# Mask products of two score steps issued together in four 32-row groups, in a routed-attention and hard-swish kernel

## Chip, cores and metric

The kernel runs on one core of one Trainium2 chip. The metric is the device time of one execution in microseconds, the median of several executions. The engines have the names of the profile: PE is the matrix engine (PEld its loads of weights), DVE the vector engine, ACT the scalar engine, POOL the third elementwise engine, SP the engine that issues most of the DMA transfers.

## What is computed

Routed attention over 4 batches of 8 heads, 768 positions, 64 dimensions per head, followed by a two-layer block with a hard-swish. A query sees the keys of its own cluster alone; the cluster of a row is the one of 16 normalised centroids with the largest product.

```python
q_assign = np.argmax(np.einsum('bhsd,hcd->bhsc', q_n, c_n), axis=-1)
k_assign = np.argmax(np.einsum('bhsd,hcd->bhsc', k_n, c_n), axis=-1)
mask = q_assign[:, :, :, None] == k_assign[:, :, None, :]
scores = np.where(mask, scale * np.matmul(q, k.transpose(0, 1, 3, 2)), -1000000000.0)
attn = np.exp(scores - np.max(scores, axis=-1, keepdims=True))
attn = attn / (np.sum(attn, axis=-1, keepdims=True) + 1e-09)
x = np.matmul(attn, v)            # then (B, H, S, D) -> (B*S, H*D) = (3072, 512)
h = x @ w_in                      # w_in is 512 x 2048
out = (h * np.clip(h + 3.0, 0.0, 6.0) / 6.0) @ w_out
```

## The kernel before

The 32 heads are handled as 16 pairs (`g`): two heads of a pair lie in the two halves of the 128 partitions, `t` = 0 in rows 0 to 63 and `t` = 1 in rows 64 to 127. The first eight pairs (`FIRST` = 8) are "unsorted": their scores are taken in full, 768 by 768, and masked. The last eight are sorted by cluster first and take only bands of the scores; they have their own functions (`band_scores` and others) and are not touched by the change.

The unsorted pairs run in 96 steps `n`, 12 for a pair: step `n` handles one half of the queries (`hf`, 384 of them) and one chunk of 128 keys (`j`) for both heads. Its scores stand in a PSUM tile `ps` of two banks, one bank per head. `psum_s` has two such tiles, so the tile of step n is the one that step n-2 had, and is free when the exponential of step n-2 has read it.

The mask is added to the scores by a product of its own. `route` makes one-hot rows of the clusters (`one_hot`, 128 positions by 12 chunks by 128 columns, of which each head uses 16 out of 64), where a query's row has a one in its cluster and a key's row has ones everywhere else; `route_turn` turns these rows on PE into `xm`, whose rows are clusters and whose columns are positions, the keys' part scaled by -2^60. The product of `xm`'s keys and queries is then 0 for a pair of one cluster and -2^60 for others. It is bfloat16 and has 64 rows per head. The product of the queries and keys themselves (`xf`) is fp32 and also has 64 rows per head. In the profile each fp32 matmul appears as two records, a bf16 one as one record.

`scores(n)` issues, for one step, the two mask products (one per head, `start=True`) and the two score products onto the same banks (`stop=True`). In the first step of a pair (`hf == j == 0`) the score products come first, through `scores_qk`, since `xm` is not ready yet; for the first pair that holds for steps 0 and 1.

The main loop takes two steps at a time (`for n in range(0, total + lag_d + 2, 2)`), and everything is issued in the order in which it is written (`manual_schedule`): each engine works through its own instructions in that order. A round of the loop holds, in this order: `scores`, `exponentials` (ACT, L423) and `key_sums` (POOL, L433) of steps n and n+1; `attn_v` (L443) of steps n-2 and n-1; every sixth step the sum over keys and its reciprocal (`sum_up`, L467, L473); then preparation for the next pair, by the round's place `r` in its pair: `turn` (transposes of q and k, L320) at r = 0 and 2, `cluster_scores` (L337) at r = 4, `route` (L348 to L357) at r = 6, `route_turn` (L379) at r = 8 and 10; and steps that decode the weights of the two layers from their 64-bit form (L228 to L259), mostly on DVE, some on ACT. From step 56 on, products of the first layer for a finished batch (L597) are put between the rounds. After the 96 steps comes the long part (the sorted pairs between the products of the two layers, L645 and L684), which lasts until the end.

The functions that the change touches are `route`, `scores` and, new, `masks`.

Of the kernel before, what the change touches and what calls it, by code (L numbers as in the profile page):

```python
# [8 lines left out]
F32 = mybir.dt.float32  # L9
# [4 lines left out]
ACT = mybir.ActivationFunctionType  # L14
# [3 lines left out]
C = 16  # L18
P = 128
NCH = S // P  # L20
NC2 = 2 * NCH
HALF = S // 2
NHC = NCH // 2
# [96 lines left out]
def fast_path(ctx, tc, ok, q, k, v, centroids, moe_w_in, moe_w_out, out):  # L120
# [3 lines left out]
    nc = tc.nc  # L124
# [32 lines left out]
    psum_s = whole.enter_context(tc.tile_pool(name="psum_s", bufs=2, space=PSUM))  # L157
# [10 lines left out]
    one_hot = nump.tile([P, NC2, P], BF16, name="one_hot")  # L168
# [9 lines left out]
    st = {}  # L178
    later = []

    def scratch(shape, name, dtype=F32):

        if st["early"]:
            return psum_m.tile(shape, dtype, name=name, tag="m")
        return psum_t.tile(shape, dtype, name=name, tag="t")
# [158 lines left out]
    def route(g):  # L344
        cs = st.pop(("cs", g))
        pr = scratch([P, NC2, 2, C], "pr")
        for i in range(NC2 // 4):
            nc.tensor.transpose(out=pr[:, 4 * i : 4 * i + 4], in_=cs[:, i], identity=ident)  # L348
        pr = pr.rearrange("p j t c -> p (j t) c")
        mx = rtp.tile([P, 2 * NC2], F32, name="mx")  # L350
        nc.vector.reduce_max(out=mx, in_=pr, axis=AX.X)
        oh = one_hot.rearrange("p j (t c) -> p j t c", t=2)[:, :, :, 0:C]
        pr = pr.rearrange("p (j t) c -> p j t c", t=2)
        mx = mx.rearrange("p (j t) -> p j t", t=2)
        halves = [slice(0, NCH), slice(NCH, NC2)]
        for sl, op in zip(halves, (ALU.is_ge, ALU.is_lt)):
            nc.vector.tensor_tensor(  # L357
                out=oh[:, sl], in0=pr[:, sl],
                in1=mx[:, sl].unsqueeze(3).to_broadcast([P, NCH, 2, C]), op=op,
            )  # L360


        def count():
            for a, sl in enumerate(halves):
                seen = rtp.tile([P, NCH, 2, C], BF16, name="seen")
                nc.scalar.activation(
                    out=seen, in_=oh[:, sl], func=ACT.Copy, scale=1.0 - 2 * a,
                    accum_out=counts[:, a, g : g + 1],
                )

        later.append(count)
# [16 lines left out]
    def where(n):  # L388
        g, r = divmod(n, 2 * NCH)
        return (g, *divmod(r, NCH))  # L390

    def scores_qk(n):
        st["ps", n] = psum_s.tile([P, 2, 512], F32, name="ps")
        scores_part(n, st["xf", where(n)[0]], True, False)

    def scores_part(n, x, first, last, onto=False):
        g, hf, j = where(n)
        for t in range(2):
            r = slice(t * D, (t + 1) * D)
            nc.tensor.matmul(  # L400
                st["ps", n][:, t, 0:HALF], lhsT=x[r, NCH + j],
                rhs=x[r, hf * NHC : (hf + 1) * NHC], start=first, stop=last,
                skip_group_check=onto,
            )

    def scores(n):
        g, hf, j = where(n)
        if ("ps", n) not in st:  # L410
            if hf == j == 0:
                scores_qk(n)
            else:
                st["ps", n] = psum_s.tile([P, 2, 512], F32, name="ps")
                scores_part(n, st["xm", g], True, False)
                scores_part(n, st["xf", g], False, True)
                return
        scores_part(n, st["xm", g], False, True)

    def exponentials(n):  # L420
        sc = st.pop(("ps", n))[:, :, 0:HALF]
# [772 lines left out]
    def prep_items(g, r):  # L1194

        if g > FIRST:
            return []
        turns = [lambda part=part: turn(g, part) for part in range(3)]
        if g == FIRST:
            return {  # L1200
                0: turns[:2], 2: turns[2:], 4: [lambda: cluster_scores(g)], 6: [lambda: own_clusters(g)],
            }.get(r, [])
        one_hots = [lambda: route_turn(g, 0), lambda: route_turn(g, 1)]
        return {
            0: turns[:2], 2: turns[2:], 4: [lambda: cluster_scores(g)], 6: [lambda: route(g)],
            8: one_hots[:1], 10: one_hots[1:],
        }.get(r, [])
# [38 lines left out]
    with tc.manual_schedule():  # L1246
# [12 lines left out]
        cluster_scores(0)  # L1259
        scores_qk(0)  # L1260
        route(0)
        scores_qk(1)
        for part in range(2):
            route_turn(0, part)

        for n in range(0, total + lag_d + 2, 2):
            g, r = divmod(n, per_pair)
            steps = [i for i in (n, n + 1) if i < total]
            prep = prep_items(g + 1, r)
            for i in steps:  # L1270
                scores(i)
                exponentials(i)
                key_sums(i)
# [359 lines left out]
@with_exitstack  # L1633
def kernel(
    ctx: ExitStack,
    tc: tile.TileContext,
    q: bass.AP,
    k: bass.AP,
    v: bass.AP,
    centroids: bass.AP,  # L1640
    moe_w_in: bass.AP,
    moe_w_out: bass.AP,
    out: bass.AP,
):
    ins = (q, k, v, centroids, moe_w_in, moe_w_out)
    flagp = ctx.enter_context(tc.tile_pool(name="flagp", bufs=1))
    ok = flagp.tile([1, 1], I32, name="ok")
    with ExitStack() as inner:
        good = fast_path(inner, tc, ok, *ins, out)
    with tc.If(good == 0):  # L1650
        with ExitStack() as inner:
            general_path(inner, tc, *ins, out)
# [32 lines left out]
```

## Time and profile before

| | us |
|---|---|
| median of three executions | 969.6 |
| lowest and highest of them | 968.26, 972.77 |
| the profiled execution | 966.25 |
| span of the profiled execution, first to last instruction | 964.5 |
| PE busy | 937.2 |
| DVE busy | 593.6 |
| POOL busy | 575.9 |
| ACT busy | 351.7 |

The profile is of one execution. "Busy" is the union of an engine's instructions in time. A row of a group of instructions has the source line, the engine, the operation, what it writes and reads, the tile of the matrix engine in use (64*128 is 64 rows by 128 columns), the shapes, the count, then the time in us covered by the group and the mean duration of one in ns, and last the time that the engine stood idle just before such instructions, with what ended it. A row of the timeline has the start in us, the length in us, the engine, the instruction, the count of instructions merged into the row, and in brackets the idle time before it. Matmuls overlap in their pipeline, so a row's length is longer than the time until the next can start: the distance of two starts is the time that a group takes on PE.

### The profile page before, as it was taken

What the parts mean: (1) busy time and instruction counts of PE and PEld (TensorE: products, weight loads), DVE (VectorE), ACT (ScalarE), POOL (GpSimd) and SP (SyncE); (2) the same over time, 40 slices, a digit from 0 to 9 for tenths busy, and PEclk for the clock granted to TensorE, in tenths of its full rate; (3) what the DMA queues carried; (4) which work ended last, traced back from release to release, by engine and by line L of the source; (5) the groups of instructions that cost most, each with busy time, mean ns of one, the idle gap of its engine ahead of it and who ended that gap; (6) DMA issues with size and microseconds to landing.
All of it is one profiled execution on the core that took longest, in us unless ns stands there. A gap on an engine that the chain in (4) does not pass through costs nothing.

```text
span 964.5 us, 17602 instructions
## 1 busy us (share of the span) xinstructions
PE 937.2 (97%) x6358; PEld 724.8 (75%) x6358; DVE 593.6 (62%) x1306; ACT 351.7 (36%) x715; POOL 575.9 (60%) x1302
## 2 busy tenths in 40 slices
PE   8999999999899999999999999899999999999997
PEld 5444445455798797797887888778788799999996
DVE  6789888989985375384483473464473464626261
ACT  6888887865112232232132141241231311202020
POOL 3878767657366577877777868767787150303030
PEclk9999999999999999999999999999999999999999
DMA  7345454340474467375583574753744333323220
GB/s 200 95 132 154 132 175 128 107 138 11 157 234 121 119 180 157 103 193 123 165 201 100 141 177 128 169 138 102 185 145 108 99 97 112 105 70 106 58 64 26
DMA packets 174351, 124.23 MB, mean 129 GB/s; under 512 B 134064, under 2 KB 152496, under 8 KB 174256
## 3 DMA queue, kind: packets, MB, share of 16 engines
q1 hardware_dynamic: 164320, 109.86, 42.7%
q0 software_dynamic: 9216, 12.60, 4.3%
q8 instruction: 52, 0.85, 0.4%
q10 hardware_dynamic: 720, 0.56, 0.2%
q14 instruction: 43, 0.35, 0.1%
HBM read 94.67 MB, written 28.31 MB: 128 GB/s over the span
## 4 chain that ended last, share of the span: by engine, by line
PE 62%; POOL 4%; DMA 3%; DVE 3%; issue 1%; ACT 0%; SPq 0%; DVEq 0%; POOLq 0%; ACTq 0%
PE Y L684 16%; PE uY L645 13%; PE X L684 11%; PE uX L645 10%; PE ps L1060 4%; PE pv L1080 3%; DMA piece<-qd 3%; PE ps L899 2%; POOL kvd L1014 1%; POOL qd L1014 1%; POOL w_low L1006 1%; DVE tx L556 1%; PE pd L1104 1%; PE ps L1121 1%; DMA xn<-xsd,pos 0%
## 5 line engine op out<-in xcount | busy, mean ns | idle before, releaser
L433 POOL TENSOR_TENSOR acc<-acc,ex 128x768 f32<-128x768 f32 x64 | 123.4, 1927 | 37.4 <-ACT ex L423 33.9
L1014 POOL DMA_INDIRECT qd<-qn,pos x96 | 96.9, 1010 | 62.3 <-DVE pos L997 22.3
L1030 POOL DMA_INDIRECT xn<-xsd,pos x96 | 93.8, 977 | 46.5 <-ACT sx L499 25.1
L499 ACT ACTIVATE sx<-g_sb,half_c 128x512 f32<-128x512 f32 x88 | 63.5, 721 | 141.2 <-DVE g_sb L656 137.2
L635 POOL TENSOR_TENSOR g_sb<-g_sb 128x256 f32<-128x256 f32 x52 | 41.8, 824 | 122.1 <-DVE g_sb L502 121.1
L1014 POOL DMA_INDIRECT kvd<-kvn,pos x96 | 95.8, 998 | 26.1 <-issue 26.1
L1006 POOL MEMSET w_low<- 128x1 f32 x864 | 91.1, 105 | 33.3
L691 DVE TENSOR_TENSOR y<-y,Y 128x256 f32<-128x256 f32 x48 | 20.2, 421 | 132.3 <-PE Y L684 131.5
L684 PE MATMUL X<-w_out_sb,g_sb 128*128 128x256 f32 x384 | 90.5, 382 | 4.0 <-DVE y L691 2.2
L645 PE MATMUL uX<-xb,w_in_sb 128*128 128x128 f32 x704 | 93.0, 275 | 0.0
L684 PE MATMUL Y<-w_out_sb,g_sb 128*128 128x256 f32 x384 | 89.0, 381 | 0.0
L684 PE MATMUL Y<-T,g_sb 128*128 128x256 f32 x384 | 88.7, 381 | 0.0
L645 PEld LDWEIGHTS uX<-xb,w_in_sb 128*128 128x128 f32 x704 | 85.7, 192 | 0.0
L684 PEld LDWEIGHTS X<-w_out_sb,g_sb 128*128 128x128 f32 x384 | 70.9, 190 | 17.6 <-issue 3.1
L684 PEld LDWEIGHTS Y<-T,g_sb 128*128 128x128 f32 x384 | 71.8, 190 | 13.2 <-issue 4.0
L684 PEld LDWEIGHTS Y<-w_out_sb,g_sb 128*128 128x128 f32 x384 | 71.6, 190 | 12.8 <-issue 3.8
L400 PE MATMUL ps<-xf 64*128 64x384 f32 x384 | 78.5, 487 | 0.7 <-ACT ex L423 0.7
L656 DVE TENSOR_TENSOR sx<-uX,sx 128x128 f32<-128x128 f32 x176 | 51.0, 290 | 43.2 <-ACT sx L663 31.0
L423 ACT ACTIVATE ex<-ps 128x768 f32<-128x768 f32 x96 | 72.6, 803 | 4.6 <-PE ps L400 4.5
L443 PE MATMUL pv<-ex,vt 128*64 128x384 f32 x384 | 72.5, 499 | 0.0
L1064 ACT ACTIVATE be<-ps 128x768 f32<-128x768 f32 (+1 forms) x48 | 35.5, 739 | 88.9 <-PE ps L1060 57.7
L656 DVE TENSOR_TENSOR g_sb<-uY,sx 128x128 f32<-128x128 f32 (+1 forms) x176 | 65.6, 415 | 0.0
(186 smaller groups left out, 1803.4 us busy)
## 6 DMA issues: line engine op xcount, KB each, us to landing
tx<-td SPq DMA_DIRECT2D x86, 384.0 KB
raw<-in_moe_w_in_dram SPq DMA_DIRECT2D x16, 512.0 KB
raw<-in_moe_w_out_dram SPq DMA_DIRECT2D x16, 512.0 KB
xb<-xd SPq DMA_DIRECT2D x12, 512.0 KB
out_dram<-y SPq DMA_DIRECT2D x44, 128.0 KB
qk<-in_q_dram SPq DMA_DIRECT2D x18, 192.0 KB
qk<-in_k_dram SPq DMA_DIRECT2D x18, 192.0 KB
vt<-in_v_dram SPq DMA_DIRECT2D x16, 192.0 KB
```

The source lines that it names most:

```text
L400: nc.tensor.matmul(st["ps", n][:, t, 0:HALF], lhsT=x[r, NCH + j], rhs=x[r, hf * NHC : (hf + 1) * NHC], start=first, stop=last, skip_group_ ...
L423: nc.scalar.activation(out=ex, in_=sc, func=ACT.Exp, scale=SM_SCALE)
L433: nc.gpsimd.tensor_tensor(out=acc, in0=acc, in1=ex, op=ALU.add)
L443: nc.tensor.matmul(pv[t * D : (t + 1) * D], lhsT=vt[:, t, j], rhs=ex[:, t], start=(j == 0), stop=(j == NCH - 1),)
L499: nc.scalar.activation(out=r, in_=h, func=ACT.Relu, bias=half_c, scale=1.0 / 6.0)
L635: eng.tensor_tensor(out=out_, in0=in0, in1=in1, op=op)
L645: nc.tensor.matmul(dst, lhsT=w[:, kt], rhs=x(kt), start=(kt == 0), stop=(kt == HK - 1))
L656: nc.vector.tensor_tensor(out=out_, in0=in0, in1=in1, op=ALU.add)
L684: nc.tensor.matmul(bank[:, half * HC : (half + 1) * HC], lhsT=g_sb[:, kind, i], rhs=w[:, i], start=(first and i == 0), stop=(last and i == ...
L1006: nc.gpsimd.memset(w_low, W_LOW)
L1014: i = nc.gpsimd.indirect_dma_start(out=rows[name, g, t], in_=src, in_offset=None, out_offset=bass.IndirectOffsetOnAxis(ap=pos[:, a, j, t : ...
L1030: nc.gpsimd.indirect_dma_start(out=xn[:, j, t], out_offset=None, in_=rows["xsd", g, t], in_offset=bass.IndirectOffsetOnAxis(ap=pos[:, 0, j ...
```

## The change

`one_hot` keeps its size. Its 128 columns per chunk were two blocks of 64, one per head, with 16 in use; they become four blocks of 32, two copies `d` of (head 0, head 1), again with 16 in use each. `route` writes each of its two comparisons twice, once for each copy. After `route_turn`, which is unchanged, `xm` has the rows of head 0 at 0 to 31 and 64 to 95, those of head 1 at 32 to 63 and 96 to 127.

A new function `masks(n)`, called in the even steps, issues the mask products of steps n and n+1 together: four matmuls of 32 rows, each in a row group of its own and into a bank of its own. For this it takes the PSUM tile of step n+1 already at step n, before the score products of step n. Then `scores(n)` issues the score products of step n and `scores(n + 1)` those of step n+1. Where the score products came first (`scores_qk`), the masks are added behind them, as before.

```diff
@@ route
-        oh = one_hot.rearrange("p j (t c) -> p j t c", t=2)[:, :, :, 0:C]
+        oh = one_hot.rearrange("p j (d t c) -> p j d t c", d=2, t=2)[:, :, :, :, 0:C]
...
         for sl, op in zip(halves, (ALU.is_ge, ALU.is_lt)):
-            nc.vector.tensor_tensor(
-                out=oh[:, sl], in0=pr[:, sl],
-                in1=mx[:, sl].unsqueeze(3).to_broadcast([P, NCH, 2, C]), op=op,
-            )
+            for d in range(2):
+                nc.vector.tensor_tensor(
+                    out=oh[:, sl, d], in0=pr[:, sl],
+                    in1=mx[:, sl].unsqueeze(3).to_broadcast([P, NCH, 2, C]), op=op,
+                )
...
                 nc.scalar.activation(
-                    out=seen, in_=oh[:, sl], func=ACT.Copy, scale=1.0 - 2 * a,
+                    out=seen, in_=oh[:, sl, 0], func=ACT.Copy, scale=1.0 - 2 * a,
                     accum_out=counts[:, a, g : g + 1],
                 )
@@ scores
+    def masks(n):
+        for d in range(2):
+            g, hf, j = where(n + d)
+            begun = ("ps", n + d) in st
+            if not begun:
+                st["ps", n + d] = psum_s.tile([P, 2, 512], F32, name="ps")
+            x = st["xm", g]
+            for t in range(2):
+                r = slice((2 * d + t) * 2 * C, (2 * d + t + 1) * 2 * C)
+                nc.tensor.matmul(
+                    st["ps", n + d][:, t, 0:HALF], lhsT=x[r, NCH + j],
+                    rhs=x[r, hf * NHC : (hf + 1) * NHC], start=not begun, stop=begun,
+                )
+            st["masked", n + d] = not begun
+
     def scores(n):
         g, hf, j = where(n)
-        if ("ps", n) not in st:
-            if hf == j == 0:
+        if n % 2 == 0:
+            if hf == j == 0 and ("ps", n) not in st:
                 scores_qk(n)
-            else:
-                st["ps", n] = psum_s.tile([P, 2, 512], F32, name="ps")
-                scores_part(n, st["xm", g], True, False)
-                scores_part(n, st["xf", g], False, True)
-                return
-        scores_part(n, st["xm", g], False, True)
+            masks(n)
+        if st.pop(("masked", n)):
+            scores_part(n, st["xf", g], False, True)
```

## Prediction

> **What bounds the kernel now.** I read the page's totals first, then the busy time by stage, then the matmul groups by shape, then the timeline of PE around the score steps.
>
> ```profile
> span 964.5 us, 17602 instructions
> PE 937.2 (97%) x6358; PEld 724.8 (75%) x6358; DVE 593.6 (62%) x1306; ACT 351.7 (36%) x715; POOL 575.9 (60%) x1302
> ```
>
> ```profile
> 60.00:84.40 24.40, 24.27 (x165) 10.78 (x165) 23.25 (x27) 20.95 (x47) 18.89 (x10) 1.00 0.54 151
> ...
> 240.00:600.00 360.00, 351.96 (x2452) 293.48 (x2449) 211.56 (x573) 93.17 (x175) 255.47 (x764) 1.00 0.58 154
> 600.00:965.00 365.00, 353.96 (x2434) 313.76 (x2432) 177.19 (x490) 77.70 (x152) 155.41 (x436) 0.99 0.39 105
> ```
>
> The columns are the stretch, its length, then busy time of PE, PEld, DVE, ACT, POOL. PE is busy throughout, so time on PE counts one for one. The first row is one unsorted pair: PE 24.27 of 24.40, but DVE 23.25 and ACT 20.95 too, so here the order of waits between three engines matters. The change lies wholly in this first quarter.
>
> ```profile
> L400 PE MATMUL ps<-xf 64*128 64x384 f32 x384 | 78.5, 487 | 0.7 <-ACT ex L423 0.7
> L400 PE MATMUL ps<-xm 64*128 64x384 bf16 x192 | 30.5, 327 | 3.2 <-ACT xm L384 1.3 <-ACT ex L423 1.0 <-DVE xm L382 0.7
> ```
>
> Today PE waits hardly at all before score and mask products (0.7 and 3.2 us in all).
>
> **What is removed.** One round of two steps on PE:
>
> ```profile
> 119.85 0.85 PE L337 MATMUL pcs<-xf,cnT 128*32 128x384 f32 x8
> 120.64 0.34 PE L400 MATMUL ps<-xm 64*128 64x384 bf16 x2
> 120.81 0.81 PE L400 MATMUL ps<-xf 64*128 64x384 f32 x4
> 121.45 0.33 PE L400 MATMUL ps<-xm 64*128 64x384 bf16 x2
> 121.61 0.81 PE L400 MATMUL ps<-xf 64*128 64x384 f32 x4
> 122.35 1.51 PE L443 MATMUL pv<-ex,vt 128*64 128x384 f32 x8
> ```
>
> From start to start, the two mask products of a step, side by side in two row groups of 64, take 121.61 - 121.45 = 0.16 us together. If four groups of 32 run side by side as two do, a round needs 0.16 once, not twice: 48 rounds x 0.16 = 7.7 us less. No row shows four row groups. The row nearest to it is the first of this fence: eight fp32 records in four column groups take 0.79 us, two records each at 0.32 (half of 0.64, below) plus a changeover, so four column groups do run at once. I take four row groups as one, and keep two at a time (nothing removed) as the other end.
>
> **What is added on PE: a change of tile shape.** Score products of one step take 121.45 - 120.81 = 0.64 when the mask products of the same shape follow. When `pv` of another shape (128*64) follows, 122.35 - 121.61 = 0.74. So a change of shape holds PE for 0.10 us. Behind a change the first weights are not loaded ahead either, as the first step of a pair shows, where score products come directly after transposes:
>
> ```profile
> 58.94 0.92 PE L400 MATMUL ps<-xf 64*128 64x384 f32 x4
> 59.91 0.50 PE L400 MATMUL ps<-xm 64*128 64x384 bf16 x4
> 60.25 0.81 PE L400 MATMUL ps<-xf 64*128 64x384 f32 x4
> 60.99 1.51 PE L443 MATMUL pv<-ex,vt 128*64 128x384 f32 x8
> ```
>
> 0.92 against 0.81: 0.11 us for fp32 weights. Now the masks are 64*128 like the scores, and the step from one to the other is free. Behind the change the masks are 32*128 and the scores 64*128: one changeover more per round, 0.10 + 0.11 = 0.21 us, in 47 rounds (in the first, scores come before both masks): 9.9 us. In a pair's first round the extra change from scores to masks falls into the wait for `xm` (58.94 to 59.91 is 0.97, not 0.74). That no row has 32-row groups leaves the ends 0 (no changeover between row groups) and about 0.3 (four weight loads of the masks one behind the other, 0.03 us each by a row shown below, 0.11 for four). I take 0.21, as rows of three other shapes agree on the 0.10.
>
> [...]
>
> Balance on PE alone: +9.9 - 7.7 = **+2.2 us**.
>
> **What is moved: the wait for the exponential.** `masks(n)` writes the tile of step n+1, which the exponential of step n-1 must have left. Before, PE asked for that 0.8 us later, behind the score products of step n. Everything on PE is queued behind it: score products, `pv`, transposes. ACT is often late, since decoding and copies stand before its exponentials. The release itself takes 0.05 us:
>
> ```profile
> 123.91 1.49 ACT L423 ACTIVATE ex<-ps 128x768 f32<-128x768 f32 x2
> ...
> L423 ACT ACTIVATE ex<-ps x96: 787/799/856, 14.3 to 234.4; 128x768 f32<-128x768 f32 x96
> ```
>
> ```profile
> 124.75 0.34 PE L400 MATMUL ps<-xm 64*128 64x384 bf16 x2 [0.41 <-ACT ex L423]
> ```
>
> The first of the two exponentials ends at 123.91 + 0.79 = 124.70, and PE, which waited, starts at 124.75. The second ends at 125.40: the new wait here is 125.40 + 0.05 - 124.75 = 0.70. Two more, from one pair:
>
> ```profile
> 59.05 0.81 ACT L384 ACTIVATE xm<-po 128x768 bf16<-128x768 bf16 x1 [0.57 <-PE po L379]
> 62.53 1.49 ACT L423 ACTIVATE ex<-ps 128x768 f32<-128x768 f32 x2
> 71.93 0.48 ACT L342 COPY cs<-pcs 128x384 f32<-128x384 f32 x1 [1.11 <-PE pcs L337]
> 74.27 1.49 ACT L423 ACTIVATE ex<-ps 128x768 f32<-128x768 f32 x2
> ```
>
> ```profile
> 63.45 0.34 PE L400 MATMUL ps<-xm 64*128 64x384 bf16 x2
> 75.43 0.34 PE L400 MATMUL ps<-xm 64*128 64x384 bf16 x2
> ```
>
> 62.53 + 1.49 + 0.05 - 63.45 = 0.62, and 74.27 + 1.49 + 0.05 - 75.43 = 0.38. Both can fall due in one pair, for ACT's work is tied to PE: at 59.05 and again at 71.93 ACT had idled until PE gave it `po` and `pcs`, and is busy without a gap from there to the exponentials. A PE that is later makes ACT later by as much. (Between the two, at 67.85, a lack of 0.48 is covered by the 0.62 just lost.) Over the 48 rounds I find 12 such waits; the first and the last:
>
> ```profile
> 14.31 1.51 ACT L423 ACTIVATE ex<-ps 128x768 f32<-128x768 f32 x2 [0.52 <-PE ps L400]
> 190.16 1.49 ACT L423 ACTIVATE ex<-ps 128x768 f32<-128x768 f32 x2
> ```
>
> ```profile
> 15.39 0.34 PE L400 MATMUL ps<-xm 64*128 64x384 bf16 x2
> 191.37 0.34 PE L400 MATMUL ps<-xm 64*128 64x384 bf16 x2
> ```
>
> 0.48 and 0.33. Worked out alike for the rest (0.11, 0.33, 0.45, 0.33, 0.60, 0.70, 0.45), the 12 sum to 5.5 us. PE arrives some 0.05 us later in each by its own balance: **+4.9 us**. Ends: 2 us, if ACT catches up more between the waits; 7.4 us without the changeover, for then PE arrives 0.21 earlier at each.
>
> **What is added on DVE.** Two comparisons more per pair:
>
> ```profile
> 12.02 0.62 DVE L357 TENSOR_TENSOR one_hot<-pr,mx 128x192 bf16<-128x192 f32 x2
> 13.32 0.56 DVE L382 TENSOR_SCALAR xm<-po 128x768 bf16<-128x768 bf16 x1 [0.67 <-PE po L379]
> ...
> 78.70 0.62 DVE L357 TENSOR_TENSOR one_hot<-pr,mx 128x192 bf16<-128x192 f32 x2
> ```
>
> ```profile
> 13.93 0.11 PEld L400 LDWEIGHTS <-xm 64*128 64x128 bf16 x4 [0.83 <-DVE xm L382]
> ```
>
> Two take 0.62, so a pair's two more take some 0.55, 4.4 us over eight pairs. In the first pair nothing else is left to do: comparisons, transposes, `xm`, masks wait on each other, so PE loses **+0.5 us** there. Later the cover is that PE is itself later by over 1 us a pair (waits and changeovers), which leaves DVE, short by 24.40 - 23.25, the time it needs. Without that cover the transposes at r = 8 wait for the comparisons, and up to 3.9 us more fall due.
>
> POOL, the DMA queues and the 192 mask matmuls with their weight loads are the same in number; no transfer is moved.
>
> **Does the loss reach the end?** The chain of waits behind 240 us runs over DVE and POOL for a time:
>
> ```profile
> 244.32 1.67 DVE T L523
> ...
> 306.98 2.30 DMA qd<-qn,pos
> 309.30 2.97 DMA piece<-qd
> ```
>
> ```profile
> 229.15 0.69 DVE L502 SCALAR_TENSOR_TENSOR g_sb<-g_sb,ph 128x512 f32<-128x512 f32 x1 [0.51 <-ACT g_sb L499]
> ```
>
> It starts from DVE work that had waited, through ACT, for PE at 229.15, so it moves with PE, and everything behind it too. I count the loss in full.
>
> **Sum.** 2.2 + 4.9 + 0.5 = +7.6 us against the profiled execution's 966.25 (span 964.5, the rest around it): 973.9. The median of the runs shown, 969.6, is 3.35 above that execution; on it the forecast is **977 us**, slower by 0.8%. Its own range, from waits of 2 us to waits with DVE's 3.9, is 974 to 982.
>
> **Rivals.**
> *Faster: the packing pays.* No changeover between 64-row and 32-row groups, and ACT early enough. Then -7.7 + 0.5 = -7.2: 962 us. For it: going between the two score tiles' own row groups costs nothing now, and every changeover in the trace also changes the columns or goes to 128 rows. Against it: the 12 rows above, in which the exponential ends too late. It decides if PE shows no gap between masks and scores and under 1 us of new waits.
> [...]
> *Nothing to measure.* No changeover, but the waits grow to 7.4: -7.7 + 7.4 + 0.5 = +0.2, 970 us; or the changeover stays and ACT catches up wholly: +2.7, 972 us.
> *The change doesn't do what it says.* The four groups run two at a time, 7.7 back: 2.2 + 7.7 + 4.9 + 0.5 = +15.3, 985 us. For it: two is all that the trace shows in rows. Against it: four column groups do run at once.
> *DVE becomes the bound.* 23.25 of 24.40 us in a pair is nearly that; +3.9 on the forecast, 981 us. Against it: PE's own lateness gives DVE the time.
>
> **How the numbers follow.** Forecast 0.54, faster 0.13, nothing to measure 0.18, two at a time 0.09, DVE 0.06. What a measurement tells from no change is about 0.5%, 4.8 us: below 964.8 faster, above 974.4 slower. The last two cases are slower, and so is the forecast but for its lowest edge (0.03): slower 0.66, same 0.21, faster 0.13. The range that leaves 2 in 10 out cuts the faster case (0.13) and the upper part of two at a time: 966 to 985 us.
>
> **What would show it.** In the changed profile: mask rows of shape 32*128, four records, with starts a few ns apart; 0.16 us from them to the next group if free, 0.26 with the changeover, and score rows of 0.92 or so in place of 0.81, for two steps at 1.28 + 0.11 on PE. Idle time before the masks ended by the exponentials (L423), from 0.7 + 1.0 us now to about 5 to 7. Twice as many comparison rows on DVE, and in the first pair masks 0.5 us later. The end of the 96 steps some 7 us later, the long part as long as before. The forecast is wrong if the masks-to-scores step stays at 0.16, or if ACT ends its exponentials in time although PE did not slow down.

## The result

The changed kernel takes 975.95 us (median of six, 975.31 to 978.19), the kernel before 968.15 us (median of six): 7.8 us more, a ratio of 1.0079 with a 95% interval of 1.0055 to 1.0102. The forecast was 977, 7.6 us above its own base of 969.6 (the median of the three executions shown before it).

The profile of the changed kernel, its totals and the matmul groups of the first 260 us by shape:

```profile
span 974.5 us, 17619 instructions
PE 943.1 (97%) x6358; PEld 723.4 (74%) x6358; DVE 597.4 (61%) x1322; ACT 352.4 (36%) x715; POOL 577.8 (59%) x1302
```

```profile
L401 PE MATMUL ps<-xf 64*128 64x384 f32 x384 | 77.1, 513 | 0.6 <-ACT ex L436 0.6
...
L418 PE MATMUL ps<-xm 32*128 32x384 bf16 x192 | 19.9, 330 | 4.7 <-ACT ex L436 2.4 <-ACT xm L385 1.3 <-DVE xm L383 0.7
```

The mask products are as many as before (192), now 32*128, and cover 19.9 us instead of 30.5: the packing is real. PE is nevertheless busy for 943.1 us instead of 937.2. Two rounds of the changed kernel in the timeline of PE, the first with the new wait, and ACT's exponentials in that round:

```profile
63.76 1.09 PE L320 MATMUL pqk<-ident,qk 128*128 128x128 f32 x8
64.78 0.33 PE L418 MATMUL ps<-xm 32*128 32x384 bf16 x2
65.36 0.34 PE L418 MATMUL ps<-xm 32*128 32x384 bf16 x2 [0.25 <-ACT ex L436]
65.63 1.56 PE L401 MATMUL ps<-xf 64*128 64x384 f32 x8
67.12 1.51 PE L456 MATMUL pv<-ex,vt 128*64 128x384 f32 x8
...
69.80 0.34 PE L418 MATMUL ps<-xm 32*128 32x384 bf16 x4
70.07 1.56 PE L401 MATMUL ps<-xf 64*128 64x384 f32 x8
71.56 1.51 PE L456 MATMUL pv<-ex,vt 128*64 128x384 f32 x8
```

```profile
63.82 1.49 ACT L436 ACTIVATE ex<-ps 128x768 f32<-128x768 f32 x2
```

The second of these rounds in the kernel before, its first and last row:

```profile
67.85 0.34 PE L400 MATMUL ps<-xm 64*128 64x384 bf16 x2
...
69.57 1.51 PE L443 MATMUL pv<-ex,vt 128*64 128x384 f32 x8
```

The undisturbed round takes 71.56 - 69.80 = 1.76 us from masks to `pv`; before, the same round took 69.57 - 67.85 = 1.72. Its masks need 0.27 until the scores start (0.16, and 0.10 for the change of shape), and its scores 1.49 where two of the 0.64 and one changeover would be 1.38: 0.11 for weights that are not loaded ahead (PEld begins to load them at 70.07, with the scores; in the kernel before at 67.85, 0.17 ahead of the scores at 68.02). In the round before it the second pair of masks stands 0.58 us behind the first, and starts 0.05 us after the exponentials end at 63.82 + 1.49 = 65.31. The idle time in brackets (0.25) is shorter than that wait, for the first pair's row covers the first 0.33 us of it. Since the four products start together where nothing is waited for, the whole 0.58 is lost, and a list of idle time shows under half of it.

### The profile page after: what moved, and what is told of

The parts are those of the page before. It is cut to its first block, busy times and chain, and to the rows that moved or that the text cites. A ratio compares the mean times of both kernels' runs of the same rounds, so it can differ in the third digit from the quotient of the medians.

```text
span 974.5 us, 17619 instructions
## 1 busy us (share of the span) xinstructions
PE 943.1 (97%) x6358; PEld 723.4 (74%) x6358; DVE 597.4 (61%) x1322; ACT 352.4 (36%) x715; POOL 577.8 (59%) x1302
## 4 chain that ended last, share of the span: by engine, by line
PE 58%; POOL 7%; DVE 4%; DMA 2%; issue 2%; SPq 0%; ACT 0%; POOLq 0%; DVEq 0%
PE Y L697 14%; PE uY L658 14%; PE uX L658 10%; PE X L697 10%; PE ps L1073 4%; PE pv L1093 3%; POOL kvd L1027 2%; PE ps L912 2%; POOL qd L1027 2%; DMA piece<-qd 2%; POOL w_low L1019 2%; DVE tx L569 1%; PE pd L1117 1%; PE ps L1134 0%; PE pcs L337 0%
## 5 line engine op out<-in xcount | busy, mean ns | idle before, releaser
L704 DVE TENSOR_TENSOR y<-y,Y 128x256 f32<-128x256 f32 x48 | 20.2, 421 | 131.8 <-PE Y L697 130.9
```

## The experiments

Since executions differ by about 1 us at the start and by some us in the long part, three times are used below: from the start of the first mask product to the start of the last product of key sums (`pd`) of the unsorted pairs ("the 96 steps"), from there to the end ("the long part"), both from one profile, and the ratio of the times to the kernel before on the same chip. The runs of this section came after the first comparison, on three chips, and on each of them the kernel before takes 963.3 to 963.8 us, some 4.5 less than in the first; whether the first was on another chip again is not on record.

| kernel | the 96 steps, us | the long part, us | ratio to before (95%) |
|---|---|---|---|
| before, first comparison | 227.00 | 723.5 | |
| changed, first comparison | 233.38 | 727.2 | 1.0079 (1.0055 to 1.0102) |
| before_again | 227.05 | 720.2 | 0.9999 (0.9988 to 1.0009) |
| after_again | 233.38 | 723.1 | 1.0093 (1.0079 to 1.0107) |
| joint64 | 230.20 | 720.4 | 1.0032 (1.0021 to 1.0043) |
| apart32 | 244.28 | 721.2 | 1.0187 (1.0173 to 1.0201) |
| twice_dve | 227.57 | 723.2 | 1.0028 (1.0018 to 1.0038) |
| exp_first | 230.83 | 720.8 | 1.0050 (1.0037 to 1.0063) |
| exp_xm_first | 230.56 | 725.8 | 1.0083 (1.0068 to 1.0098) |
| before_exp_first | 227.30 | 720.1 | 1.0005 (0.9996 to 1.0014) |
| scores_first | 227.63 | 724.8 | 1.0031 (1.0020 to 1.0043) |
| scores_exp_first | 227.92 | 720.5 | 1.0024 (1.0015 to 1.0034) |
| after_turn_later | 233.37 | 716.8 | 1.0020 (1.0011 to 1.0029) |
| before_turn_later | 227.01 | 716.1 | 0.9941 (0.9928 to 0.9954) |

The 96 steps repeat to a few hundredths of a microsecond in three profiles of either kernel's steps (the kernel before, before_again, before_turn_later; the changed one, after_again, after_turn_later); the change costs 6.35 us there. The long part does not repeat.

**The wait alone: joint64.** In the kernel before:

```diff
+    def masks(n):
+        for d in range(2):
...
+            scores_part(n + d, st["xm", g], not begun, begun)
+            st["masked", n + d] = not begun
     def scores(n):
...
-                scores_part(n, st["xm", g], True, False)
+        if n % 2 == 0:
...
+            masks(n)
+        if st.pop(("masked", n)):
             scores_part(n, st["xf", g], False, True)
```

> The kernel before, with the mask products of both steps of a round issued together ahead of the score products, as in the change, but in the two row groups of 64: no packing, no change of tile shape, no second copy of the comparisons. Only the wait for the exponential of step n-1 moves forward. Theory (waits): the twelve waits of the prediction, each 0.16 us shorter because the second step's masks come 0.16 us behind the first's, so 5.5 - 1.9 = 3.6 us more: about 971.8 us, and idle time before the mask products ended by the exponentials. Rival (ACT catches up, the loss is all changeover): no change, 968 us.

Measured: 3.2 us more in the 96 steps, 3.1 us in the median, so the theory holds. Twelve rounds are longer, by 3.7 us in all (3.6 were expected), and 0.5 comes back between rounds, where PE's own waits became shorter. The timeline of PE and ACT at the place quoted above:

```profile
64.00 0.34 PE L400 MATMUL ps<-xm 64*128 64x384 bf16 x2
64.60 0.34 PE L400 MATMUL ps<-xm 64*128 64x384 bf16 x2 [0.26 <-ACT ex L429]
64.76 1.47 PE L400 MATMUL ps<-xf 64*128 64x384 f32 x8
66.16 1.51 PE L449 MATMUL pv<-ex,vt 128*64 128x384 f32 x8
```

```profile
63.06 1.49 ACT L429 ACTIVATE ex<-ps 128x768 f32<-128x768 f32 x2
```

The same wait without any 32-row group: 64.60 is 0.05 after 63.06 + 1.49, and 0.44 later than the 0.16 that the first pair needs. With scores of the same shape behind, 64.76 - 64.60 is 0.16 and the two steps' scores take 1.40, without the 0.10 and 0.11. Asking for the tile earlier costs PE time by itself.

**The changeover alone: apart32.** In the changed kernel, each step's masks ahead of its own scores:

```diff
-            masks(n)
-        if st.pop(("masked", n)):
+        x, d = st["xm", g], n % 2
+        for t in range(2):
+            r = slice((2 * d + t) * 2 * C, (2 * d + t + 1) * 2 * C)
+            nc.tensor.matmul(
...
+        if not begun:
             scores_part(n, st["xf", g], False, True)
```

> The changed kernel, with each step's two 32-row mask products issued just ahead of its own score products: the wait stands where it stood before, nothing is packed, and a round changes tile shape between 32 and 64 rows three times more than before. Theory (a changeover costs 0.10 us, and 0.11 more into fp32 weights): 0.21 + 0.11 + 0.21 = 0.53 us in each of 40 rounds, 0.05 in the seven first rounds of a pair, 0.5 at the start: 22 us more, about 990 us. Rival (row groups of 32 and 64 follow each other freely, the loss is all waits): 0.5 us more, 968.7 us.

Measured: 17.2 us more in the 96 steps, 18.1 in the median. One round on PE:

```profile
68.97 0.33 PE L419 MATMUL ps<-xm 32*128 32x384 bf16 x2
69.24 0.92 PE L401 MATMUL ps<-xf 64*128 64x384 f32 x4
70.09 0.34 PE L419 MATMUL ps<-xm 32*128 32x384 bf16 x2
70.35 0.92 PE L401 MATMUL ps<-xf 64*128 64x384 f32 x4
71.20 1.51 PE L449 MATMUL pv<-ex,vt 128*64 128x384 f32 x8
```

The round takes 71.20 - 68.97 = 2.23 where it took 1.72: 0.51 for the expected 0.53. No wait for exponentials is in it. Going from 32 to 64 rows costs 0.10 and then 0.11, from 64 to 32 rows 0.10 (0.85 from scores to masks is 0.64 + 0.11 + 0.10). All 40 rounds that were counted lose 0.50 or 0.51, 20.2 us with the first rounds of the pairs. The sum is less since 2.9 us come back at seven places between the rounds: there PE had waited for something in the kernel before, and it waits less when it comes later. Free passage between row groups is refuted.

**The comparisons alone: twice_dve.** In the kernel before:

```diff
-        oh = one_hot.rearrange("p j (t c) -> p j t c", t=2)[:, :, :, 0:C]
+        oh = one_hot.rearrange("p j (t d c) -> p j t d c", t=2, d=2)[:, :, :, :, 0:C]
...
+            for d in range(2):
                 nc.vector.tensor_tensor(
-                    out=oh[:, sl], in0=pr[:, sl],
+                    out=oh[:, sl, :, d], in0=pr[:, sl],
```

> The kernel before, with each comparison of the one-hot rows written twice (the second copy into unused columns of the same 64, so the mask is -2^61 instead of -2^60) and nothing else changed. Theory: 0.5 us more, in the first pair alone, 968.6 us. Rival (DVE, busy 95% of a pair, is the bound): up to 4.4 us more, 972.5 us.

Measured: 2.3 us more, between the two expectations. The 96 steps lose 0.57 us, nearly all of it (0.53) in one round, where the transposes at r = 8 of the third pair wait for the comparisons. The rest is in the long part, where this profile has two slow stretches that the profile of before_again lacks: from 619.00 to 622.40 us the granted clock is 0.50 (1.00 in before_again from 617.20 to 621.00), and 8 products at 260.00 us take 3.26 us instead of 1.99 (last section). So DVE is not the bound in the steps. That its later end brings on the slow stretches is not shown: they come and go in other kernels too, and the kernel before, without a second copy, was granted 0.50 from 617.43 to 620.84 us in its first profile, and 1.00 near there in before_again.

**ACT's order: exp_first, exp_xm_first, before_exp_first.** In the main loop, the decoding steps and range checks of a round are kept and issued behind the next round's `attn_v`:

```diff
+            for step in held:
+                step()
+            check_all()
...
-            if n < total:
-                for step in decode[: share(n, r)]:
-                    step()
-                del decode[: share(n, r)]
-            check_all()
+            held = decode[: share(n, r)] if n < total else []
+            del decode[: len(held)]
```

> The changed kernel, with a round's steps of weight decoding and range checks issued behind the exponentials and value products of the next round instead of ahead of them; the order on DVE and the DMA queue stays, on ACT the exponentials come first. Theory (the new waits come from ACT work ahead of the exponentials): most of the 5.3 us of waits go, the changeovers stay, so about 971 us, with the last key-sum product of the unsorted pairs near 242.5 us instead of 247.3. Rival (the loss lies in PE's own work or in the long part behind): 976 us as the changed kernel.

Measured: the steps lose 3.8 us instead of 6.35, the median 5.2 us. PE's waits in the first 250 us, by whom:

```profile
PE ps L418 <- ACT xm L385: 4.5, 6, 1.3
...
PE ps L418 <- ACT ex L436: 0.3, 1, 0.3
```

The distances between the two pairs of masks, which idle time understates, sum to 1.4 us where they were 5.2, so ACT's work ahead of the exponentials caused most of the wait. What is left is 0.64 in the first round, where ACT itself had waited for PE, and 0.32, 0.32 and 0.16 in three others. But the copies of `xm` now stand behind the decoding: 1.3 us of waits became 4.5. ACT's lateness was moved, less than half of the loss saved.

> The kernel before with the round's decoding steps and range checks behind the next round's exponentials. Theory (the kernel before waits for exponentials in 4 places, 1.7 us, and for xm, which this order makes later by some 3 us as it did in the changed kernel): 1 to 3 us more, 965 to 967 us where the kernel before takes 964. Rival (PE gains from earlier exponentials): 1 to 2 us less.

Measured: no change (+0.6 us, and the interval of the ratio includes 1), 0.3 us in the steps. Neither of the two: PE's waits for exponentials (1.6 us) are gone, those for `xm` rose from 1.3 to 4.3, and other waits between the rounds became shorter as PE came later.

> The changed kernel with decoding steps and range checks behind the next round's exponentials, and in the rounds that turn the one-hot rows (r = 8 and 10) behind the copies of xm too. Theory (changeovers 2.2 us and the first pair's 0.5 us are what is left when neither exponentials nor xm come late): 2.7 us more than the kernel before, with the last key-sum product near 243.5 us. Rival (the long part or DVE takes the gain back): 5 us more, as with the exponentials alone ahead.

Measured: 3.5 us more in the steps, 8.5 in the median, so neither expectation is met. The wait for `xm` is back at 0.3, but exponentials keep 1.8 and a transpose waits 1.6 for DVE's reciprocal; and the long part begins badly, on PE:

```profile
265.41 3.78 PE L697 MATMUL X<-w_out_sb,g_sb 128*128 128x256 f32 x8 [5.17 <-DVE y L704]
```

DVE's `y` for the second layer comes late (5.17 us of waiting, 2.22 in the kernel before), and the 8 products take nearly twice as long (3.78 us; 1.99 in the kernel before). That the decoding, pushed further back, makes DVE late there fits the edit, but was not tested alone.

**Scores first: scores_first, scores_exp_first.** In the changed kernel:

```diff
         if n % 2 == 0:
-            if hf == j == 0 and ("ps", n) not in st:
-                scores_qk(n)
+            for d in range(2):
+                if ("ps", n + d) not in st:
+                    scores_qk(n + d)
             masks(n)
-        if st.pop(("masked", n)):
-            scores_part(n, st["xf", g], False, True)
```

(in `masks`, `start=False, stop=True`)

> The changed kernel with the order turned round inside a round: score products of both steps first, then the four packed mask products on top of them. Packing, changeovers and the second copies stay as many; the tile of step n+1 is asked for 0.75 us later, about as late as in the kernel before. Theory (waits and changeovers are separate costs that add): the waits of 5.3 us go, 2.2 us of changeovers and 0.5 us in the first pair stay: the rounds lose 0.04 us each and no more, the last key-sum product near 243.5 us, and 3 us more than the kernel before, 966.5 to 967. Rival (the waits only move, since the exponentials can now start later by 0.85 us): 6 us more as with the changed kernel.

Measured: 0.6 us more in the steps, 3.3 in the median. One round on PE:

```profile
67.85 1.56 PE L401 MATMUL ps<-xf 64*128 64x384 f32 x8
69.34 0.34 PE L415 MATMUL ps<-xm 32*128 32x384 bf16 x4
69.61 0.87 PE L450 MATMUL pv<-ex,vt 128*64 128x384 f32 x4
```

1.76 us, as in the changed kernel: packing and changeover are still there and still lose 0.04 us a round. But the four mask products stand together in all 48 rounds, so the 5.2 us are gone; 1.7 us of waits for exponentials are left, ahead of the scores, and the kernel before had 1.6. The steps end even better than expected, for in the first round of a pair the second step's scores fill the wait for `xm`: 0.3 to 0.7 us in each of seven, 3.0 in all, of which 1.6 is lost again in longer waits between the rounds. The waits are therefore separate from the changeovers, and the order inside the round decides them.

> Score products ahead of the packed masks, and also the decoding steps and range checks behind the next round's exponentials. Theory: the exponentials are no longer what PE waits for once the scores stand first, so the second edit adds nothing to the first but the later xm copies it cost elsewhere: 1 to 3 us more than with the scores first alone. Rival (ACT's lateness still counts): 1 to 2 us less than with the scores first alone.

Measured: 0.3 us more in the steps than with the scores first alone (4.1 us of waits for `xm`). The median is 0.5 us less, which the intervals of the two ratios do not tell apart. The second edit does nothing for the steps.

**The long part: before_again, after_again, after_turn_later, before_turn_later.**

> The kernel before once more, unedited, for a profile on this chip beside the others of this call. Every theory: no change, within 0.3%, the last key-sum product of the unsorted pairs near 241 us. It shows how much of the long part's length differs from chip to chip.

> The changed kernel once more, unedited. Theory (all of the loss arises before the last key-sum product, 6.4 us, and the rest of the difference in the first pair of profiles was between two executions): 6 to 8 us more than the kernel before on this chip, the long part within 1 us of the kernel before. Rival (the change lengthens the long part by 3.7 us, as the first two profiles have it): 10 us more.

Measured: the kernel before as expected; of the changed kernel the steps as in the first comparison, 9.0 us more in the median, and the long part 2.9 us longer than before (3.7 in the first), so the theory that it stays within 1 us fails. PE near the place where the difference between these two arises, before_again and after_again:

```profile
617.25 0.85 PE L899 MATMUL ps<-ident,piece 128*128 128x128 f32 x6 [2.35 <-DMA piece<-qd]
617.94 0.61 PE L645 MATMUL uY<-xs,tx 128*128 128x128 f32 x4
```

```profile
625.35 1.51 PE L912 MATMUL ps<-ident,piece 128*128 128x128 f32 x6 [3.44 <-DMA piece<-qd]
626.65 1.06 PE L658 MATMUL uY<-xs,tx 128*128 128x128 f32 x4
```

and the busy time by stretches there (stretch, length, PE, PEld, DVE, ACT, POOL, then the granted clock of PE), after_again:

```profile
614.00:625.30 11.30, 7.91 (x61) 6.55 (x60) 5.88 (x20) 1.62 (x4) 8.99 (x29) 0.99 0.66 147
625.30:629.00 3.70, 3.65 (x20) 3.69 (x21) 0.00 (x0) 0.80 (x1) 3.11 (x11) 0.58 1.02 233
629.00:640.00 11.00, 11.00 (x96) 9.22 (x96) 8.63 (x28) 4.08 (x8) 4.00 (x14) 1.00 0.78 198
```

A load of ranked queries is late, PE waits 3.44 us instead of 2.35, and then runs at a lower clock (0.58 granted on the mean from 625.30 to 629.00 us; 1.00 in before_again from 617.20 to 621.00): from these transposes to the next ones, at 629.27 and 619.72, it takes 3.92 us instead of 2.47. 1.1 + 1.45 = 2.5 us, most of the difference in the long part. The first comparison is another matter: there both profiles have the wait (3.12 and 3.60 us) and a half-clock stretch at it (0.50 granted from 617.43 to 620.84 us and from 629.24 to 632.64), and 3.4 of the 3.7 us had come up before, from 359 to 494 us of the kernel before, in steps of 0.2 to 0.7 us, about half of it (1.9) at transposes of loaded pieces. What set these off is not shown. To see how much of the total lies there, the transposes of the loaded pieces were put one place later, in either kernel:

```diff
-            (-4, load_ranked, 2), (-3, turn_ranked, 0), (-2, turn_ranked, 1),
+            (-4, load_ranked, 2), (-2, turn_ranked, 0), (-1, turn_ranked, 1),
```

> The changed kernel with the two transposes of ranked queries and keys of each sorted pair one place later in the long part, so that their loads have some 2 us more. Theory (the part of the difference that lies in the long part comes from PE's wait for these loads, 7.2 us in all, and from the halved clock behind a wait of over 3 us): the waits fall under 1 us each and no half-clock stretch stands near 625 us; 5 to 7 us less than the changed kernel, 966 to 968. Rival (the wait only moves to the band scores behind): no change.

> The kernel before with the same two transposes one place later. Theory: 4 to 6 us less than the kernel before, 958 to 960 us, and the gap to the changed kernel with the same edit is what arises in the unsorted pairs alone, 6 to 7.5 us. Rival (the wait moves to the band scores): no change.

Measured: 965.06 us for the changed kernel with this edit, 957.99 us for the kernel before with it. PE's waits for this load in the long part, in the two:

```profile
PE ps L912 <- DMA piece<-qd: 1.6, 1, 1.6
```

```profile
PE ps L899 <- DMA piece<-qd: 1.0, 1, 1.0
```

From 7.2 and 6.2 us (six waits each) to one wait. In before_turn_later the transposes at 615.89 us take 0.85 us, as they did in before_again with 1.00 granted; the clock at this place in after_turn_later is not shown. The long part is 716.8 and 716.1 us, and the gap is 965.06 - 957.99 = 7.1 us. So the change costs 7.1 us with this edit: 6.35 in the steps, about half a microsecond at the start (worked out below), and under one in the long part. Against the expectation, each kernel keeps one wait for the load, of 1.6 and 1.0 us, and the changed kernel gains 7.8 us against after_again where 5 to 7 were expected. What the other two comparisons show beyond 7.1 us lies in the long part, in waits for these loads and, in the second, in the clock. Before_turn_later beats both kernels: 0.9941 (0.9928 to 0.9954) of the kernel before.

## Why the prediction was right, step by step

- **What is removed.** Right: four row groups run at once. In the round at 69.80 the four mask products are one row of 0.34, start within 0.01 us of each other, and the scores follow 0.27 behind. The rival that they run two at a time falls.
- **The changeover.** Right in price: 0.10 and 0.11, as the rows of other shapes had it. Per round it leaves 0.04 us of loss instead of the 0.05 forecast (1.76 against 1.72): 47 x 0.04 - 0.16 = 1.7 for the forecast 2.2 us. apart32 shows the price alone (0.51 a round), against the rival by which the packing pays.
- **The wait for the exponential.** Right: the second pair of masks stands apart from the first in exactly the 12 rounds that the prediction counted, by 5.2 us in all, for the forecast 4.9. In nine of them it is up to 0.06 shorter than the prediction's value, as forecast, in two the same 0.70, since PE had waited there before too, and in the first 0.64 instead of 0.48. joint64 shows the wait without the rest (3.2 us), exp_first takes away most of its cause, scores_first the wait itself. That ACT is tied to PE, so that one pair can pay twice, is shown by the 0.58 at 64.78 and another of 0.33 at 77.47 in the same pair.
- **What the sum left out.** 5.2 + 1.7 would be 6.9; the steps lost 6.35. Some of PE's own waits of before became shorter, since PE comes later. The largest, in the kernel before and in the changed one:

```profile
183.20 0.66 PE L320 MATMUL pqk<-ident,qk 128*128 128x128 f32 x4 [0.76 <-DVE rcp L473]
```

```profile
188.99 0.66 PE L320 MATMUL pqk<-ident,qk 128*128 128x128 f32 x4 [0.25 <-DVE rcp L486]
```

- **DVE's comparisons.** Right for the first pair. The cover named for the later pairs was hardly needed: twice_dve, whose PE comes no later, loses 0.57 us there, not the "up to 3.9" that the prediction set for a kernel without cover. The four comparisons and what follows on DVE and PE in the changed kernel:

```profile
11.56 1.15 DVE L358 TENSOR_TENSOR one_hot<-pr,mx 128x192 bf16<-128x192 f32 x4
13.31 0.56 DVE L383 TENSOR_SCALAR xm<-po 128x768 bf16<-128x768 bf16 x1 [0.60 <-PE po L380]
```

```profile
13.93 0.34 PE L418 MATMUL ps<-xm 32*128 32x384 bf16 x4 [0.65 <-DVE xm L383]
```

  From comparisons to masks it is 13.93 - 11.56 = 2.37 us, before it was 13.93 - 12.02 = 1.91: 0.46 for the forecast 0.5. This execution happened to begin its comparisons 0.46 earlier, so the masks themselves do not stand later, and the mark named in the prediction ("masks 0.5 us later") did not show. Over all 14 profiles the first masks start between 13.49 and 14.82 us, a scatter larger than this effect.
- **"I count the loss in full."** Right for the steps. That the long part stays as long did not hold: it was 3.7 and 2.9 us longer in the profiles. Of the 7.8 us of the first comparison, 6.35 + 0.46 = 6.8 leave 1.0 to the long part and to chance; of the 9.0 us of after_again, 2.2. The sum had neither the waits that became shorter nor the longer long part, and these two pull in opposite directions (0.55 less, about 1.0 more), so part of its closeness is luck. (The upper end of its own range, 982, is also 1 us above its own terms: 969.6 + 7.6 + 3.9 = 981.1.)

Of the rivals, "nothing to measure" had one thing right without happening: the wait can be taken away (scores_first), and then little is left.

## What to carry to other kernels

Packing matmuls into more row groups pays only if it saves more than the changes of tile shape around it cost: here 0.16 us was saved per round and 0.21 paid to change the shape and load fp32 weights behind it. Issuing the products of two steps together also asks for both steps' buffers at the time of the first, so count the slack of the second buffer against the engine that frees it, and put first the product that can use the earlier buffer while the other comes free. A sum made stage by stage should be checked stage by stage: here the total hid a long part that varied by as much as half the effect.

## What the runs showed of the hardware that was not expected

PE also ran slow behind a wait of 2.22 us, and not each time. In the first profiles of the two kernels the granted clock was 0.50 for 3.41 us at waits of 3.12 and 3.60 us, and the stretch at 625 us above came with a wait of 3.44 us. In twice_dve the 8 products at 260.00 us came behind a wait of 2.22 us and took 3.26 us; the same wait in before_again brought nothing of the kind (the 8 products took 1.99), nor did it in the first profiles (1.99 in both). Twice_dve first:

```profile
260.00 3.26 PE L685 MATMUL X<-w_out_sb,g_sb 128*128 128x256 f32 x8 [2.22 <-DVE y L692]
```

```profile
259.28 1.99 PE L684 MATMUL X<-w_out_sb,g_sb 128*128 128x256 f32 x8 [2.22 <-DVE y L691]
```

What decides is not shown. The length of the wait alone does not: 2.22 us went with both, and behind 2.35 us in before_again the granted clock was 1.00. Nor does the low clock start with the end of the wait: in the kernel before it starts at 617.43 us, 0.45 ahead of that end (617.88), in the changed one at 629.24, 1.02 behind it (628.22). In each of these two profiles it is granted once more, behind PE's last product, and the two starts are a whole number of the 3.413 us of the first stretch apart: 617.43 and 962.18 us in the kernel before (344.75, 101.0 times), 629.24 and 970.57 in the changed one (341.33, 100.0 times).
